# One unit's transposes in 64-row halves, another unit's second product in float32 by two column halves

## Chip, cores and metric

The kernel runs on one core of a Trainium2 chip. The metric is the device time of one execution in microseconds (us); lower is better.

## What is computed

Clustered attention and two dense blocks behind it, in float32. Queries and keys (2 batches, 8 heads, 768 positions, 64 wide) are each put to the nearest of 16 centroids of their head; a query sees the keys of its own cluster.

```python
mask = q_assign[:, :, :, None] == k_assign[:, :, None, :]
scores = np.where(mask, scale * np.matmul(q, k.transpose(0, 1, 3, 2)), -1000000000.0)
attn = np.exp(scores - np.max(scores, axis=-1, keepdims=True))
attn = attn / (np.sum(attn, axis=-1, keepdims=True) + 1e-09)
x = np.matmul(attn, v)                      # then (1536, 512)
h = np.maximum(x @ w_in, 0.0)
x = h * h @ w_out                           # first block, d_ff 2048
h = x @ w2_in
out = (h * np.clip(h + 3.0, 0.0, 6.0) / 6.0) @ w2_out
```

## The kernel before

Precision comes from splitting: a float32 operand is kept as a rounded high part and the remaining low part, both of the type fp32r, and a product is made of high by high, high by low and low by high.

The attention is done in 8 units, each one batch and two heads. A unit has 12 tiles: for each head 6 tiles of 128 queries against all 768 keys. Three tiles make a group, with 384 queries. For tile `n` the steps are

- `emit_qk` (L901, L904): the scores, two products of 384 columns by two terms, the second term with the mask rows;
- `emit_max` (L910, DVE) and `emit_exp` (L921, ACT, with a record that reads the accumulated sum): the exponentials `e` of [128 queries, 768 keys] in float32;
- `emit_tr` (L939): `e` transposed by PE in six blocks of 128 x 128, three for each `half` of the keys, into a bank of PSUM (`t`, three buffers that other steps share). The half is then split into `eh` and `el` either by ACT and DVE (L949, L950), or, for the tiles in `ON_POOL`, by a copy `et` (ACT, or DVE for `ET_DVE`) and two POOL operations (L377, L947);
- `emit_av` (L966): for each chunk `part` of 128 keys two products, the stationary operand being V's high and low parts side by side (64 + 64 columns), the moving one `eh`, then `el`; `emit_u` adds the two halves of the output's partitions.

The order is written out by hand. `schedule` runs for each tile `n` the places 0, 1, 1.5, 1.7, 2, 3, 4; between them stand `emit_tr(n, 0)` (after place 0), `emit_exp(n + 1)`, `emit_qk(n + 2)`, `emit_max(n + 2)` and `emit_tr(n, 1)` (after place 2). The tables `STEPS` and `FIRST` give the tile and place of each preparation step (loads, transposes of q and k `tq`, similarities `tsim`, their transposes `tas` of 64 rows, one-hot rows `toh`, mask rows `mt`, V's split in `vsplit`, the final scaling with `tn`), and `AV` gives the places of a group's six parts and of `emit_u`, counted from the group's first tile:

```python
AV = ((3, 3), (3, 4), (4, 1.7), (5, 0), (5, 1.7), (5, 2), (5, 2))
```

Each engine works through its instructions in this order. The loads and the transfers that build the stacked operands `op` all go through SP's queue. The steps of unit 0 stand in `OPENING`, with fill products on PE (`idle`, L783; `IDLE = (2, 3, 4)` gives their number at three places). Behind the attention the two dense blocks follow, in an order set by a planner (`Plan`), which the diff does not touch.

Of the kernel before, what the change touches and what calls it, by code (L numbers as in the profile page):

```python
# [9 lines left out]
F32 = mybir.dt.float32  # L10
F32R = mybir.dt.float32r
# [5 lines left out]
I32 = mybir.dt.int32  # L17

WARM = 10
FILL = {(0, 0): 1, (0, 1): 1, (1, 0): 1, (1, 1): 1, (2, 0): 1, (2, 1): 2, (3, 0): 2, (3, 1): 2}  # L20
IDLE = (2, 3, 4)

# [61 lines left out]
        "norm1": (17, 0),  # L84
    },
    2: {
        "load q": (-18, 1.5),
        "load k": (-17, 2),
        "load v": (-8, 1),
        "sim0": (-11, 0),  # L90
# [237 lines left out]
def cluster_attention_mlp_kernel(  # L328
# [38 lines left out]
    def f(ap):  # L367
        return ap.bitcast(F32)
# [78 lines left out]
    with ExitStack() as actx:  # L447
# [116 lines left out]
        def prep(u):  # L564
# [172 lines left out]
            def vsplit(half):  # L737
                if half == 0:
                    vst[u] = vs_p.tile([P, R, 2, 2 * D], F32R, tag="vs", name="vs")
                hs = slice(3 * half, 3 * half + 3)  # L740
                vr = raw[u, "v"][:, hs].rearrange("p r h d -> p (r h) d")
                tt = vst[u][:, hs].rearrange("p r h d -> p (r h) d")
                if E_VH == "p":
                    pool_round(tt[:, :, 0:D], vr)
                elif E_VH == "v":
                    nc.vector.tensor_copy(tt[:, :, 0:D], vr)
                else:
                    nc.scalar.activation(tt[:, :, 0:D], vr, AF.Copy)
                (nc.gpsimd if E_VL == "p" else nc.vector).tensor_sub(tt[:, :, D:], vr, f(tt)[:, :, 0:D])
# [20 lines left out]
            def first():  # L770

                h = ((0, 3), (3, 6))
                held = {}

                def hold(k, fn, *args):
                    held[k] = fn(*args)

                def idle(n):
                    if not n:
                        return  # L780
                    wt = ps_t.tile([P, 512], F32, tag="t", name="warm")
                    for _ in range(n):
                        nc.tensor.matmul(  # L783
                            wt[:, :HS], C[:, 0, 0:P], st["H"][:, 0, :HS], start=True, stop=True
                        )

                def table():
                    warm = sm_p.tile([P, 1], F32, tag="warm", name="warm", bufs=1)
                    nc.scalar.activation(warm, three, AF.Exp)

                steps = {
                    "q0": lambda: hold("q0", transp, 0, 0, True),
                    "cent": lambda: centroid_operands(cent),
                    "q0 split": lambda: held.pop("q0")(),
                    "k0": lambda: hold("k0", transp, 1, 0, True),
                    "k0 split": lambda: held.pop("k0")(),
                    "q1": lambda: hold("q1", transp, 0, 1, True),
                    "q1 split": lambda: held.pop("q1")(),
                    "k1": lambda: hold("k1", transp, 1, 1, True),
                    "k1 split": lambda: held.pop("k1")(),  # L800
                    "sim00": lambda: sims(0, 0),
                    "sim01": lambda: sims(0, 1),
                    "sim10": lambda: sims(1, 0),
                    "sim11": lambda: sims(1, 1),
                    "stack0": lambda: stack(0),
                    "stack1": lambda: stack(1),
                    "load k": lambda: load(1, "k"),
                    "load v": lambda: load(0, "v"),
                    "table": table,
                    "assign0": lambda: assign(*h[0]),  # L810
                    "lead0": lambda: leader(*h[0], 0),
                    "hot0": lambda: onehot(*h[0], 0),
                    "mask0": lambda: mask0(*h[0]),
                    "assign1": lambda: assign(*h[1]),
                    "lead1": lambda: leader(*h[1], 0),
                    "hot1": lambda: onehot(*h[1], 0),
                    "mask1": lambda: mask0(*h[1]),
                    "near0": lambda: emit_qk(0, 0),
                    "near1": lambda: emit_qk(1, 0),
                    "score0": lambda: emit_qk(0, 1),  # L820
                    "score1": lambda: emit_qk(1, 1),
                    "max0": lambda: emit_max(0),
                    "max1": lambda: emit_max(1),
                    "exp0": lambda: emit_exp(0),
                    "next q0": lambda: hold("next q0", prep_step, 1, "q0"),
                    "next q0 split": lambda: held.pop("next q0")(),
                    "next q1": lambda: hold("next q1", prep_step, 1, "q1"),
                    "next q1 split": lambda: held.pop("next q1")(),
                    "idle a": lambda: idle(IDLE[0]),
                    "idle b": lambda: idle(IDLE[1]),  # L830
                    "idle c": lambda: idle(IDLE[2]),
                }
                for k in OPENING:
                    steps[k]()
# [91 lines left out]
        def emit_tr(n, half):  # L926
            u, i, r = tile_of(n)
            g = n // 3
            if n % 3 == 0 and half == 0:
                eg[g] = (  # L930
                    eg_p.tile([P, R, HS], F32R, tag="eh", name="eh"),
                    eg_p.tile([P, R, HS], F32R, tag="el", name="el"),
                )
# [6 lines left out]
            qs = slice((n % 3) * P, (n % 3) * P + P)  # L940
            ks = slice(half * 3, half * 3 + 3)
            eh, el = eg[g][0][:, ks, qs], eg[g][1][:, ks, qs]
            if (n % (2 * R), half) in (ON_POOL_FIRST, ON_POOL_SECOND, ON_POOL, ON_POOL_LAST)[u if u < 2 else 3 if u == NU - 1 else 2]:
                et = e_p.tile([P, 3, P], F32, tag="et", name="et")
                copy((n % (2 * R), half) in (ET_DVE_FIRST, ET_DVE_SECOND, ET_DVE, ET_DVE_LAST)[u if u < 2 else 3 if u == NU - 1 else 2], et, t)
                pool_round(eh, et)
                nc.gpsimd.tensor_sub(el, et, f(eh))  # L947
            else:
                nc.scalar.activation(eh, t, AF.Copy)  # L949
                nc.vector.tensor_sub(el, t, f(eh))  # L950
            if half == 1:
                E_t.pop(n)

        A_t = {}

        def emit_av(g, part):

            u, i, r = tile_of(3 * g)
            if part == 0:
                A_t[g] = ps_a.tile([P, 512], F32, tag="a", name="a")  # L960
            a = A_t[g]
            eh, el = eg[g]
            vs = vst[u]
            for kr in (part,):
                for x in (eh, el):
                    nc.tensor.matmul(  # L966
                        a[:, :HS], vs[:, kr, i, :], x[:, kr, :],
                        start=(kr == 0 and x is eh), stop=(kr == R - 1 and x is el),
                    )
# [951 lines left out]
```

## Time and profile before

| what | us |
|---|---|
| median of 3 runs (lowest to highest) | 762.22 (761.32 to 763.06) |
| the profiled execution, its own time | 762.97 |
| its span, first to last instruction | 761.2 |
| PE busy | 751.7 |
| DVE, ACT, POOL busy | 606.3, 515.4, 481.4 |
| granted clock of TensorE, mean | 1.000 |

The span lies 1.8 us under the execution's own time. In the rows, PE is the matrix engine and PEld its loading of the stationary operand, which overlaps; the ends of PE's instructions are modelled, so starts say more than busy time.

### The profile page before, as it was taken

To read this page: it belongs to the slowest core of one execution; us is meant where nothing else is said; L and a number is where in the kernel's file an instruction comes from. 1 tells how busy PE (TensorE), PEld (TensorE's weight loads), DVE (VectorE), ACT (ScalarE), POOL (GpSimd) and SP (SyncE) were. 2 spreads that over 40 slices of the span, in tenths; PEclk is the share of its full clock that TensorE was granted. 3 is DMA by queue.
4 is the path that set the end of the run, shared out by engine and by line. 5 is a ranking of instruction groups with operands and counts; after the bars stand their busy time and mean duration, and the time that the engine had idled before them with its cause. 6 is when DMAs were issued, how large, how long until landed. Compare 5 with 4: busy or idle time off the path is not lost.

```text
span 761.2 us, 13022 instructions
## 1 busy us (share of the span) xinstructions
PE 751.7 (99%) x4438; PEld 711.2 (93%) x4438; DVE 606.3 (80%) x1068; ACT 515.4 (68%) x1100; POOL 481.4 (63%) x598
## 2 busy tenths in 40 slices
PE   8989999999999999999999999999999999999998
PEld 7888999999999999999999999999999899988998
DVE  6979999999998699878678776889657777776365
ACT  5889898898998777664554545677667555564461
POOL 2767888898897589963631743799464273166433
PEclk9999999999999999999999999999999999999999
DMA  8767738648432031222212122002212223200013
GB/s 183 163 131 162 153 70 183 136 96 187 112 83 70 1 112 56 84 84 70 94 59 84 56 84 84 28 29 85 83 57 67 73 84 108 86 29 29 1 41 125
DMA packets 62353, 66.96 MB, mean 88 GB/s; under 512 B 41200, under 2 KB 42736, under 8 KB 62288
## 3 DMA queue, kind: packets, MB, share of 16 engines
q1 hardware_dynamic: 61088, 65.85, 32.1%
q8 instruction: 35, 0.57, 0.3%
q10 hardware_dynamic: 1200, 0.30, 0.2%
q14 instruction: 30, 0.25, 0.1%
HBM read 43.02 MB, written 3.15 MB: 61 GB/s over the span
## 4 chain that ended last, share of the span: by engine, by line
PE 87%; POOL 7%; ACT 2%; issue 2%; DMA 2%; DVE 0%; SPq 0%; POOLq 0%; ACTq 0%
PE b L1407 27%; PE b L1489 16%; PE b L1528 15%; PE a L966 7%; PE t L939 6%; PE s L904 3%; PE s L901 3%; PE b L1770 2%; POOL el L947 2%; PE b L1665 2%; PE tsim L646 2%; PE tq L588 1%; POOL eh L377 1%; POOL xl L1018 1%; ACT e L921 1%
## 5 line engine op out<-in xcount | busy, mean ns | idle before, releaser
L1395 DVE TENSOR_TENSOR b<-b,tmp 128x384 f32<-128x384 f32 x84 | 47.4, 566 | 76.2 <-PE b L1407 31.1
L1205 POOL TENSOR_TENSOR s<-wt,s 128x256 fp32r<-128x256 f32 (+1 forms) x68 | 69.2, 1024 | 45.6 <-ACT s L1203 37.7
L939 PE MATMUL t<-ident,e 128*128 128x128 f32 x576 | 93.4, 275 | 1.2 <-ACT e L921 0.5
L910 DVE TENSOR_REDUCE nm<-s 128x1 f32<-128x768 f32 x96 | 90.6, 944 | 2.5 <-PE s L904 2.5
L947 POOL TENSOR_TENSOR el<-et,eh 128x384 fp32r<-128x384 f32 x84 | 86.1, 1024 | 7.0
L1391 ACT ACTIVATE tmp<-b 128x384 f32<-128x384 f32 x84 | 41.2, 491 | 71.8 <-PE b L1407 71.4
L921 ACT ACTIVATE e<-s,nm 128x768 f32<-128x768 f32 x96 | 86.6, 902 | 1.6 <-DVE nm L910 0.9
L1205 POOL TENSOR_TENSOR w<-wt,w 128x256 fp32r<-128x256 f32 (+1 forms) x48 | 43.3, 911 | 61.6 <-ACT w L1203 53.9
L939 PEld LDWEIGHTS t<-ident,e 128*128 128x128 f32 x576 | 70.3, 140 | 11.4 <-ACT e L921 4.5
L1188 POOL TENSOR_SCALAR wr<-wr 128x512 f32<-128x512 f32 x60 | 40.4, 674 | 62.3 <-DMA wr<-in_moe_w_in_dram 40.9
L966 PE MATMUL a<-eh,vs 128*128 128x384 f32 x192 | 70.0, 365 | 0.4 <-POOL xh L377 0.4
L377 POOL TENSOR_SCALAR eh<-et 128x384 fp32r<-128x384 f32 x84 | 45.2, 538 | 33.3 <-ACT et L374 29.5
L1407 PE MATMUL b<-xh,s 128*128 128x384 f32 x224 | 66.2, 336 | 0.0
L1407 PE MATMUL b<-xh,w 128*128 128x384 f32 x224 | 66.2, 336 | 0.0
L966 PE MATMUL a<-el,vs 128*128 128x384 f32 x192 | 64.8, 338 | 0.1
L950 DVE TENSOR_TENSOR el<-t,eh 128x384 fp32r<-128x384 f32 x108 | 58.8, 548 | 4.8 <-ACT eh L949 3.3
L949 ACT ACTIVATE eh<-t 128x384 fp32r<-128x384 f32 x108 | 52.8, 492 | 11.4 <-PE t L939 9.7
L901 PE MATMUL s<-op 128*128 128x384 f32 x188 | 55.4, 376 | 0.0
L1377 ACT ACTIVATE tmp<-b,three 128x384 f32<-128x384 f32 x64 | 37.0, 581 | 26.7 <-DVE b L1395 22.9
L1489 PE MATMUL b<-gA,s 128*128 128x384 f32 x276 | 54.2, 334 | 0.0
L904 PE MATMUL s<-op 80*128 80x384 f32 x192 | 49.7, 339 | 2.0 <-DMA op<-mt 1.9
L1192 DVE TENSOR_SCALAR b<-wr 128x512 int32<-128x512 int32 x60 | 41.3, 688 | 13.0 <-ACT wr L1191 12.2
(268 smaller groups left out, 2217.8 us busy)
## 6 DMA issues: line engine op xcount, KB each, us to landing
wr<-in_moe_w_out_dram SPq DMA_DIRECT2D x32, 512.0 KB, 3.2
op<-HL SPq DMA_DIRECT2D x82, 192.0 KB, 4.7
wr<-in_moe_w_in_dram SPq DMA_DIRECT2D x28, 512.0 KB, 3.5
rawv<-in_v_dram SPq DMA_DIRECT2D x16, 192.0 KB, 3.9
rawq<-in_q_dram SPq DMA_DIRECT2D x14, 192.0 KB, 4.2
rawk<-in_k_dram SPq DMA_DIRECT2D x14, 192.0 KB, 4.5
wr<-in_moe_w_in_dram SPq DMA_DIRECT2D x8, 256.0 KB, 2.9
op<-xh SPq DMA_DIRECT2D x8, 192.0 KB, 4.0
```

What stands on the lines that cost most here:

```text
L901: nc.tensor.matmul(s[:, h, :HS], o[:, 0, rs], o[:, 2, hs], start=True, stop=False)
L904: nc.tensor.matmul(s[:, h, :HS], o[0:80, 1, rs], o[0:80, 3, hs], start=False, stop=True)
L910: nc.vector.tensor_reduce(nm, S_t[n][:, :, :HS], axis=AX.XY, op=ALU.max, negate=True)
L921: nc.scalar.activation(e, s[:, :, :HS], AF.Exp, bias=nm, accum_out=sums[u][:, i * R + r : i * R + r + 1])
L939: nc.tensor.transpose(t[:, c, :], E_t[n][:, half, c * P : (c + 1) * P], ident)
L947: nc.gpsimd.tensor_sub(el, et, f(eh))
L950: nc.vector.tensor_sub(el, t, f(eh))
L966: nc.tensor.matmul(a[:, :HS], vs[:, kr, i, :], x[:, kr, :], start=(kr == 0 and x is eh), stop=(kr == R - 1 and x is el),)
L1205: pool(n / 365, lambda: nc.gpsimd.tensor_sub(lo, x, f(hi)), k + hk, lk)
L1407: nc.tensor.matmul(h, w[:, a, cc], x[b][:, cc], start=(first and n == 1), stop=(n == 6 * len(terms)), skip_group_check=not first,)
L1489: nc.tensor.matmul(o, x[:, ds], y, start=(fb == 0 and k == 0), stop=(fb == NF - 1 and k == 2))
L1528: nc.tensor.matmul(o, g[:, ts], w[:, ns], start=(fb == 0 and k == 0), stop=(fb == NF - 1 and k == 2),)
```

## The change

- `emit_tr_rows` takes the place of `emit_tr` in unit 3: at place 0 of a tile all 768 keys are transposed by twelve transposes of 64 query rows each, alternating between the upper and the lower 64 rows, into two banks; each bank holds 64 queries by all 6 chunks and is split as before, with rows of 64 elements. At the place of the second half nothing is done.
- In unit 4 `emit_tr` only copies its half to `eh` (ACT for the first, DVE for the second), `vsplit` only copies V, and `emit_av_full` multiplies in float32: at the odd parts two products of 64 output columns, one chunk into output partitions 0 to 63, the next into 64 to 127. At the even parts nothing is done.
- The last four fill products of the opening become float32 products on 64 rows, alternating between the halves and between two banks.
- Unit 2's "load q" goes from tile 6, place 1.5 (18 tiles ahead of its unit) to tile 0, place 0 (24 ahead).

PE in unit 3, tiles 2 and 3 (the line numbers of the change differ). Before:

```order
L939 MATMUL t<-ident,e 128x128 x3
L901 MATMUL s<-op 128x384 x2
L904 MATMUL s<-op 128x384 x2
L966 MATMUL a<-eh,vs 128x384
L966 MATMUL a<-el,vs 128x384
L966 MATMUL a<-eh,vs 128x384
L966 MATMUL a<-el,vs 128x384
L939 MATMUL t<-ident,e 128x128 x3
L665 MATMUL tas<-ident,sim 128x64 x6
```

and in the change:

```order
L985 MATMUL t<-ident,e 128x64 x12
L915 MATMUL s<-op 128x384 x2
L918 MATMUL s<-op 128x384 x2
L1033 MATMUL a<-eh,vs 128x384
L1033 MATMUL a<-el,vs 128x384
L1033 MATMUL a<-eh,vs 128x384
L1033 MATMUL a<-el,vs 128x384
L667 MATMUL tas<-ident,sim 128x64 x6
L985 MATMUL t<-ident,e 128x64 x12
```

The second three transposes of the tile have gone to its beginning, and twelve of 64 rows stand there together; "tas", which already had 64 rows, comes to stand next to the following tile's twelve.

ACT in unit 3, from the copy of its first tile's first half on (`e,sums` is the exponential, `lo` and `tmp` belong to preparation and to `emit_u`). Before:

```order
L374 ACTIVATE et<-t 128x384
L921 ACTIVATE e,sums<-s,nm 128x768
L949 ACTIVATE eh<-t 128x3x128
L374 ACTIVATE lo<-tsim 64x384
L921 ACTIVATE e,sums<-s,nm 128x768
```

and in the change:

```order
L376 ACTIVATE et<-t 128x384
L1000 ACTIVATE eh<-t 128x6x64
L935 ACTIVATE e,sums<-s,nm 128x768
L376 ACTIVATE lo<-tsim 64x384
L1000 ACTIVATE eh<-t 128x6x64
```

The copy of the tile's second part has gone from behind the next tile's exponential to in front of it.

SP's queue in unit 0, from the load of unit 0's V on (`op<-mt` are mask rows; `op<-xh` and `op<-xl` are unit 1's stacked operands). Before:

```order
L494 DMA rawv<-in_v_dram 128x6x64 x2
L733 DMA op<-mt 16x768 x2
L621 DMA op<-xh 64x768
L622 DMA op<-xh 64x768
L623 DMA op<-xh 64x768
```

and in the change:

```order
L496 DMA rawv<-in_v_dram 128x6x64 x2
L496 DMA rawq<-in_q_dram 128x6x64 x2
L735 DMA op<-mt 16x768 x2
L623 DMA op<-xh 64x768
L624 DMA op<-xh 64x768
```

The load of unit 2's q stands ahead of unit 0's mask rows; before, it stood behind them and behind all of unit 1's stacked operands.

The diff:

```diff
--- before.py
+++ after.py
@@ -17,6 +17,8 @@
 I32 = mybir.dt.int32
 
 WARM = 10
+TR_ROWS = 3
+AV_FULL = 4
 FILL = {(0, 0): 1, (0, 1): 1, (1, 0): 1, (1, 1): 1, (2, 0): 1, (2, 1): 2, (3, 0): 2, (3, 1): 2}
 IDLE = (2, 3, 4)
 
@@ -84,7 +86,7 @@
         "norm1": (17, 0),
     },
     2: {
-        "load q": (-18, 1.5),
+        "load q": (-24, 0),
         "load k": (-17, 2),
         "load v": (-8, 1),
         "sim0": (-11, 0),
@@ -740,6 +742,9 @@
                 hs = slice(3 * half, 3 * half + 3)
                 vr = raw[u, "v"][:, hs].rearrange("p r h d -> p (r h) d")
                 tt = vst[u][:, hs].rearrange("p r h d -> p (r h) d")
+                if u == AV_FULL:
+                    nc.gpsimd.tensor_copy(f(tt)[:, :, 0:D], vr)
+                    return
                 if E_VH == "p":
                     pool_round(tt[:, :, 0:D], vr)
                 elif E_VH == "v":
@@ -779,7 +784,16 @@
                     if not n:
                         return
                     wt = ps_t.tile([P, 512], F32, tag="t", name="warm")
-                    for _ in range(n):
+                    for k in range(n):
+                        if n == 4:
+                            rs = slice(64 * (k % 2), 64 * (k % 2) + 64)
+                            if k == 0:
+                                w2 = ps_t.tile([P, 512], F32, tag="t", name="warm2")
+                            nc.tensor.matmul(
+                                (w2 if k % 2 else wt)[:, :HS], f(C)[rs, 0, 0:P],
+                                f(C).rearrange("p a b -> p (a b)")[rs, :HS], start=True, stop=True,
+                            )
+                            continue
                         nc.tensor.matmul(
                             wt[:, :HS], C[:, 0, 0:P], st["H"][:, 0, :HS], start=True, stop=True
                         )
@@ -926,6 +940,10 @@
         def emit_tr(n, half):
             u, i, r = tile_of(n)
             g = n // 3
+            if u == TR_ROWS:
+                if half == 0:
+                    emit_tr_rows(n)
+                return
             if n % 3 == 0 and half == 0:
                 eg[g] = (
                     eg_p.tile([P, R, HS], F32R, tag="eh", name="eh"),
@@ -940,7 +958,9 @@
             qs = slice((n % 3) * P, (n % 3) * P + P)
             ks = slice(half * 3, half * 3 + 3)
             eh, el = eg[g][0][:, ks, qs], eg[g][1][:, ks, qs]
-            if (n % (2 * R), half) in (ON_POOL_FIRST, ON_POOL_SECOND, ON_POOL, ON_POOL_LAST)[u if u < 2 else 3 if u == NU - 1 else 2]:
+            if u == AV_FULL:
+                copy(half, f(eh), t)
+            elif (n % (2 * R), half) in (ON_POOL_FIRST, ON_POOL_SECOND, ON_POOL, ON_POOL_LAST)[u if u < 2 else 3 if u == NU - 1 else 2]:
                 et = e_p.tile([P, 3, P], F32, tag="et", name="et")
                 copy((n % (2 * R), half) in (ET_DVE_FIRST, ET_DVE_SECOND, ET_DVE, ET_DVE_LAST)[u if u < 2 else 3 if u == NU - 1 else 2], et, t)
                 pool_round(eh, et)
@@ -951,13 +971,60 @@
             if half == 1:
                 E_t.pop(n)
 
+        def emit_tr_rows(n):
+            g = n // 3
+            if n % 3 == 0:
+                eg[g] = (
+                    eg_p.tile([P, R, HS], F32R, tag="eh", name="eh"),
+                    eg_p.tile([P, R, HS], F32R, tag="el", name="el"),
+                )
+            ts = [ps_t.tile([P, 512], F32, tag="t", name="t") for _ in range(2)]
+            for c in range(R):
+                for x in range(2):
+                    rs = slice(64 * x, 64 * x + 64)
+                    nc.tensor.transpose(
+                        ts[x][:, 64 * c : 64 * c + 64],
+                        E_t[n][rs, c // 3, (c % 3) * P : (c % 3) * P + P],
+                        ident[rs, rs],
+                    )
+            for x in range(2):
+                t = ts[x][:, :HS].rearrange("p (c q) -> p c q", c=R)
+                qs = slice((n % 3) * P + 64 * x, (n % 3) * P + 64 * x + 64)
+                eh, el = eg[g][0][:, :, qs], eg[g][1][:, :, qs]
+                if (n % (2 * R), x) in ON_POOL:
+                    et = e_p.tile([P, R, 64], F32, tag="et", name="et")
+                    copy((n % (2 * R), x) in ET_DVE, et, t)
+                    pool_round(eh, et)
+                    nc.gpsimd.tensor_sub(el, et, f(eh))
+                else:
+                    nc.scalar.activation(eh, t, AF.Copy)
+                    nc.vector.tensor_sub(el, t, f(eh))
+            E_t.pop(n)
+
         A_t = {}
+
+        def emit_av_full(g, part):
+
+            u, i, r = tile_of(3 * g)
+            a = A_t[g]
+            eh = f(eg[g][0])
+            vs = f(vst[u])
+            if part % 2 == 0:
+                return
+            for kr in (part - 1, part):
+                x = kr % 2
+                nc.tensor.matmul(
+                    a[64 * x : 64 * x + 64, :HS], vs[:, kr, i, 0:D], eh[:, kr, :],
+                    start=part == 1, stop=part == 5, skip_group_check=True,
+                )
 
         def emit_av(g, part):
 
             u, i, r = tile_of(3 * g)
             if part == 0:
                 A_t[g] = ps_a.tile([P, 512], F32, tag="a", name="a")
+            if u == AV_FULL:
+                return emit_av_full(g, part)
             a = A_t[g]
             eh, el = eg[g]
             vs = vst[u]
```

## Rows read from the trace of the kernel before

**Rows 1.** Windows, units 3, 4: us, busy us of PE, PEld, DVE, ACT, POOL.

```profile
108.30:137.84 29.54, 29.51 (x205) 27.81 (x204) 28.30 (x51) 26.87 (x61) 26.45 (x37) 1.00 0.62 137
137.84:167.40 29.56, 29.55 (x205) 27.80 (x204) 28.17 (x49) 26.88 (x61) 26.02 (x36) 1.00 0.64 137
```

**Rows 2.** Windows, unit 3, exponentials (L921) alone: two records a tile.

```profile
108.30:137.84 29.54, 11.92 (x24) 1.00 0.62 137
```

**Rows 3.** Timeline of PE in one tile of unit 3: start us, us, instructions.

```profile
122.82 0.49 PE L939 MATMUL t<-ident,e 128*128 128x128 f32 x3
123.07 0.60 PE L901 MATMUL s<-op 128*128 128x384 f32 x2
...
124.04 0.34 PE L966 MATMUL a<-el,vs 128*128 128x384 f32 x1
124.21 0.34 PE L966 MATMUL a<-eh,vs 128*128 128x384 f32 x1
```

**Rows 4.** Timeline of PE around the 64-row transposes "tas".

```profile
117.05 0.49 PE L939 MATMUL t<-ident,e 128*128 128x128 f32 x3
117.47 0.59 PE L665 MATMUL tas<-ident,sim 64*128 64x64 f32 x6
...
118.29 0.60 PE L901 MATMUL s<-op 128*128 128x384 f32 x2
```

**Rows 5.** Timeline of PEld around the same; in brackets idle time before.

```profile
117.46 0.45 PEld L665 LDWEIGHTS tas<-ident,sim 64*128 64x128 f32 x6 [0.17 <-issue]
```

**Rows 6.** Tile tas: duration ns min/median/max, first and last start.

```profile
L665 PEld LDWEIGHTS tas<-ident,sim x48: 135/138/140, 9.8 to 206.4; 64*128 64x128 f32 x48
L665 PE MATMUL tas<-ident,sim x48: 222/223/273, 9.8 to 206.5; 64*128 64x64 f32 x48
...
  issue: 1.4, 8
```

**Rows 7.** Timelines: the transposes of one half (PE), then ACT behind them.

```profile
120.11 0.49 PE L939 MATMUL t<-ident,e 128*128 128x128 f32 x3
...
120.69 0.49 ACT L374 ACTIVATE et<-t 128x384 f32<-128x384 f32 x1 [0.37 <-PE t L939]
121.08 0.90 ACT L921 ACTIVATE e<-s,nm 128x768 f32<-128x768 f32 x1
121.87 0.20 ACT L921 ACTIVATION_READ_ACCUMULATOR e<-s,nm 128x1 f32 x1
```

**Rows 8.** Opening: PE timeline, ACT timeline, and two pieces of the chain.

```profile
15.70 1.39 PE L783 MATMUL warm<-HL,c 128*128 128x384 f32 x7
...
17.11 0.55 PE L939 MATMUL t<-ident,e 128*128 128x128 f32 x3
...
16.06 0.90 ACT L921 ACTIVATE e<-s,nm 128x768 f32<-128x768 f32 x1
...
18.12 4.29 DMA rawv<-in_v_dram
...
25.72 0.79 PE a L966 x3
```

**Rows 9.** SP issues, the PE wait for the mask rows, and time to landing.

```profile
35.33 2.12 SPq L494 DMA_DIRECT2D rawq<-in_q_dram  x2
...
41.06 2.92 SPq L733 DMA_DIRECT2D op<-mt  x4
...
45.99 0.59 PE L904 MATMUL s<-op 80*128 80x384 f32 x2 [1.94 <-DMA op<-mt]
...
op<-mt SPq DMA_DIRECT2D x30, 48.0 KB, 2.2
```

**Rows 10.** Groups of the page: busy us, mean ns of one | idle us.

```profile
L939 PE MATMUL t<-ident,e 128*128 128x128 f32 x576 | 93.4, 275 | 1.2 <-ACT e L921 0.5
...
L947 POOL TENSOR_TENSOR el<-et,eh 128x384 fp32r<-128x384 f32 x84 | 86.1, 1024 | 7.0
...
L950 DVE TENSOR_TENSOR el<-t,eh 128x384 fp32r<-128x384 f32 x108 | 58.8, 548 | 4.8 <-ACT eh L949 3.3
```

## The prediction

> **What bounds the kernel now.** I read first the windows, cut at the start of each unit's exponentials. Unit 3 takes 29.54 us and unit 4 29.56 us, and PE is busy for 29.51 and 29.55 of them; DVE for about 28.2, ACT 26.9, POOL 26 [rows 1]. The stretch holds 24 records of the exponential, two a tile, so 12 tiles: 2.46 us a tile [rows 2]. A busy PE may only look full, so I then took the pitches, from start to start, out of PE's timeline. A 384-column fp32r product takes 0.17 to 0.18 us (124.04 to 124.21), say 0.175 [rows 3]. Three float32 transposes last 0.49 us as a group and 0.275 each [rows 3, 10], so the second and third add (0.49 - 0.275) / 2 = 0.11 each; that is the pitch. A tile has 6 transposes and 8 products: 0.66 + 1.40 = 2.06 us. The rest, 0.40 us a tile, is other units' preparation and merging: 18 more transposes (2.0), 8 similarity products (1.4) and a few small ones, about 4.2 us a unit. 12 x 2.06 + 4.2 = 28.9 of 29.5. **PE is the bound in both units, with about half a microsecond to spare.** What lies behind the attention is also a chain of PE, so what PE loses or gains in units 3 and 4 goes through to the end.
>
> It follows that the relief of the other engines in unit 4 is worth nothing: about half of its splits no longer have a low part on POOL (1.02 us each) and half none on DVE (0.55) [rows 10], and the float32 copy of V has one POOL operation less a half. All of that lay beside PE.
>
> **A price that the kernel before does show: changing the array's shape.** Once a unit, six transposes of 64 rows ("tas") stand among transposes of 128 rows. The three before them start at 117.05, so the array is free at 117.05 + 3 x 0.11 = 117.38. The six loads last 0.45 us as a group, 0.138 each, so the pitch is (0.45 - 0.138) / 5 = 0.062 [rows 5, 6]; they need 0.37. From the first of three transposes to the next product is 0.25 us (122.82 to 123.07) [rows 3]. So the product should start at 118.00; it starts at 118.29 [rows 4]. **0.29 us are lost by going to 64 rows and back**, and PEld stands idle 0.17 us of it for "issue", which is no wait that the profile shows; that comes 8 times, 1.4 us in all [rows 5, 6].
>
> **Unit 3, transposes.** Twelve of 64 rows take the place of six of 128 in each tile, in one go, with products on both sides. Removed: 0.66 us. Added: 0.29 for the two changes of shape, and twelve transposes. If the upper and lower half run one after the other, these are 12 x 0.062 = 0.74 us; if each pair runs at once, 0.37. No row shows two halves at work together; the only sequence of 64-row transposes has them all in one half, at 0.062 [rows 5], and I take 0.062. PE then needs 0.37 us more a tile, 12 x 0.37 = 4.5 us, less 0.29 where "tas" stands next to a burst: 4.2.
>
> There is a second cost. ACT takes its work in the order of the program. Before, one half's copy stood ahead of the next tile's exponential; now both halves do, and the next tile's transposes wait for that exponential. The loop: the last transpose of the first half starts about 0.05 + 10 x 0.062 = 0.67 us after the first and lasts 0.22 [rows 6]; the copy starts 0.09 behind it (120.60 to 120.69), 0.98; copy to copy and copy to exponential are 0.39 each (120.69 to 121.08), 1.76; the exponential with its read of the sum takes 0.99 (121.08 to 122.07) [rows 7], 2.75; the transposes start 0.06 later (the opening: 16.06 + 0.99 = 17.05 against 17.11 [rows 7, 8]). That is 2.81 us. PE alone needs 2.06 + 0.37 = 2.43 in a tile without preparation. Four tiles (0, 3, 6, 8) have none, and wait 0.38 each: 1.5 us. Before, the same loop with one copy and 3 transposes was about 2.0 us, under PE's 2.06. **Unit 3: +5.7 us**; bounds +1.9 (pairs at once, worked out below) and about +6.
>
> **Unit 4, second product.** Before, two chunks are four fp32r products, 0.70 us. Now they are two float32 products of 384 columns, with 64 output columns, and a change of shape around them: the parts 1, 3 and 5 of each group carry two chunks, so 3 bursts a group and 12 in the unit. No row shows a float32 product. Bounds: the float32 transpose costs 0.11 per 128 columns, so 0.33 for 384; and twice that, 0.66, if both operands are split in two and not only the data of a transpose. I take 0.66, nearest to the four fp32r terms (0.70) that a product of two halves by two halves would be. The Trainium skill's page "FP8 and Floating Point Precision" (TensorE Precision Notes) counts four passes for a true FP32 product, by which the sum stands as I take it. If the two chunks, in the two halves of the output's partitions, run together, a burst is 0.29 + 0.66 = 0.95, 0.25 more than before; 12 x 0.25 = 3.0 us. They also fall unevenly: one burst in the first tile of three, none in the second, two in the third. The second then has PE work of 0.66 + 0.70 = 1.36 us, less than the loop through ACT of about 2.0, which wastes some 0.1 to 0.6 a group where no preparation fills it; +0.5. **Unit 4: +3.5 us**; if the two run one after the other, 12 x 0.66 = 7.9 more, +11.4; at 0.33 and together, 0.5 - 12 x 0.08 = -0.5.
>
> **Opening.** Four fill products (0.70 us) become four float32 ones on 64 rows: two pairs, 2 x 0.66 + 0.29 = 1.6 us. The seven before began at 15.70 and the transposes at 17.11 waited for the exponential that ends at 17.05 [rows 8]; now they start some 0.6 us later (1.9 if nothing overlaps). Until 25.72 the chain runs through the load of V and POOL [rows 8], so I cost this at 0; without that cover it is 0.6 to 1.9.
>
> **The load of unit 2's q** goes from in front of the mask rows' transfers (35.33) to a place after the first load of V, where SP waits anyway. PE later waits 1.94 us for mask rows issued from 41.06 on, behind that traffic; such a transfer usually lands 2.2 us after issue [rows 9]. With 2.1 us of issues less ahead they can be earlier by 0 to 1.5 us; the mask must first be written. I take 0.8.
>
> **Sum:** 5.7 + 3.5 + 0 - 0.8 = +8.4 us on the profiled execution's 762.97 (span 761.2): 771.4. That execution lies 0.75 above the median of the runs shown, 762.22, so the forecast for a median is **770.6 us**.
>
> **Rivals.**
> - *Both kinds of halves run together.* Unit 3: PE needs 0.37 + 0.29 = 0.66 a tile as before, but ACT's loop is 2.81 - 0.37 = 2.44 against 2.06 in the four light tiles and 2.39 in five with a little preparation: 4 x 0.38 + 5 x 0.05 = 1.8. Sum 1.8 + 3.5 - 0.8 = +4.5, **766.7**. For it: the instructions alternate between the halves and write different banks. Against: 0.062 is more than half of 0.11, so part of the price may be the instruction itself, which doubles. The Trainium skill's page "TensorE: Matmul & The Clock Gate" (Part 3) gives a speed-up of about 3 for four row tiles at once, which would make this the case; no run here shows it yet.
> - *Neither runs together.* 5.7 + 11.4 + 0.5 in the opening - 0.8 = +16.8, **779.0**.
> - *Unit 4's halves one after the other, unit 3's together:* 1.8 + 11.4 - 0.8 = +12.4, 774.6.
> - *Faster: the change of shape is free when products stand on both sides*, and halves run together. Unit 3's transposes are 0.37 instead of 0.66; its loop is 2.3 us, so most of that is not used: about -0.3. Unit 4: 12 x (0.66 - 0.70) = -0.5. With 1.5 from the load: -2.3, **759.9**. It decides at a price of about 0.12 us per change and back: (24 x 0.12 is about 2.9, some of it hidden in unit 3). Against it: 0.29 in a row where nothing was waited for.
> - *The change does little*, because float32 products are cheap (0.33) and the loop through ACT is loose: within 1.5 us, 762.
>
> **Chances.** Forecast 0.40, both together 0.22, neither 0.20, mixed 0.06, faster 0.06, little 0.06. About 0.2% (1.5 us) is what a measurement of this kernel can tell from no change. So faster 0.06, same 0.06, slower 0.88. The range goes from 764.5, below the case of both together, to 780.5, over most of that of neither.
>
> **What would show it.** Right: units 3 and 4 take about 35 and 33 us, the others 29.5; in unit 3 LDWEIGHTS of 64 rows at a pitch near 0.06 in bursts of 12, "issue" before each burst, and the transposes waiting for ACT's exponential in light tiles; in unit 4 pairs of float32 products that start within 0.1 us of each other and hold PE for about 0.95 us. Wrong: a pitch near 0.03 in unit 3; float32 products 0.66 us apart (779); or no gap at the changes of shape.

## The result, and the profile after

| what | before, us | change, us |
|---|---|---|
| median of 3 runs (lowest to highest) | 762.22 (761.32 to 763.06) | 768.02 (767.90 to 769.26) |
| the profiled execution | 762.97 | 767.90 |
| its span | 761.2 | 766.1 |
| from the first exponential of unit 0 to that of unit 2 | 62.46 | 61.49 |
| unit 3 | 29.54 | 33.43 |
| units 4 and 5 together | 59.13 | 61.84 |

The change is **slower: 1.0068 times the time of before, interval 1.0043 to 1.0092**. By medians that is 5.8 us, between the two profiled executions 4.9. A unit reaches, as in [rows 1], from the start of its exponentials to that of the next unit's. Unit 4's last products fall into unit 5's window, so these two are taken together. Unit 2 is as before (29.77 after 29.78), and so is unit 6. The sum over the units: unit 3 +3.9, units 4 and 5 +2.7, units 0 and 1 together -1.0. Another 0.7 us is gained before unit 0's first exponential, ahead of everything that the change touches; that start lies between 15.4 and 16.8 us over the profiles of this study, so it is chance. Three executions of this study, the profiled one of e2 among them, took 1235 to 1903 us and enter no ratio.

The windows of the change, in the columns of [rows 1]; units 3, 4, 5:

```profile
106.62:140.06 33.44, 31.39 (x281) 26.41 (x280) 29.44 (x52) 27.27 (x63) 26.50 (x37) 1.00 0.56 121
140.06:171.15 31.09, 30.86 (x201) 23.17 (x199) 26.16 (x45) 22.94 (x51) 11.03 (x16) 1.00 0.62 130
171.15:201.90 30.75, 30.61 (x205) 25.64 (x204) 28.04 (x47) 26.39 (x61) 22.26 (x31) 1.00 0.62 132
```

Against [rows 1], PE now stands idle for 2.05 us of unit 3, where it was idle for 0.03. In unit 4 it has stayed full: POOL's work fell from 26.0 to 11.0 us and PE's time rose.

**A light tile of unit 3**, the change's answer to [rows 3]: timeline of PE and, last, the loads of PEld.

```profile
122.26 0.58 PE L985 MATMUL t<-ident,e 64*128 64x64 f32 x12
122.78 0.62 PE L915 MATMUL s<-op 128*128 128x384 f32 x2
123.23 0.51 PE L918 MATMUL s<-op 80*128 80x384 f32 x2
...
124.11 0.33 PE L1033 MATMUL a<-el,vs 128*128 128x384 f32 x1
124.68 0.58 PE L985 MATMUL t<-ident,e 64*128 64x64 f32 x12 [0.24 <-ACT e L935]
...
122.26 0.45 PEld L985 LDWEIGHTS t<-ident,e 64*128 64x128 f32 x12 [0.25 <-ACT u L396]
```

Twelve loads take 0.45 us, as long as six did in [rows 5]: **the upper and the lower half run at once**. The single records show it: the two of a pair start 3 to 4 ns apart, and twelve starts span 0.36 us. The price of the changed shape is there too. The last product before a burst is followed after 0.27 us instead of 0.175, the first pair takes 0.11 instead of 0.06, the last transpose 0.15 instead of 0.06, and the first product 0.28 instead of 0.175: 0.34 us, against the 0.29 read from "tas". A burst without waits costs six pairs at 0.062 and 0.34, together 0.71 us of PE; the six transposes of before cost 0.66. By this the form of the transposes is almost neutral, and most of the 3.9 us must be waits.

What ended the idle time of PE and of PEld before the twelve, both added up, and how often (the view of line L985):

```profile
  ACT e L935: 3.6, 8
  DVE HL L599: 1.0, 2
  issue: 0.8, 3
  ACT et L376: 0.6, 2
  DVE el L1001: 0.4, 1
```

Two things are late. One is the next tile's exponential, as at 124.68, where the transposes start 0.06 us after ACT has read the sum. The other is a **bank of PSUM**: `HL`, `et` and `el` are written by the instructions that empty a bank of `t`. The twelve transposes need two of the three banks at once, and `tq`, `tsim` and the others use the same three. In four tiles the second half starts 0.27, 0.37, 0.51 and 0.69 us after the first for want of a bank, 1.8 us together; the bank comes free with an `el`, an `et`, an `et` of unit 2's last tile, and an `HL`. PE's starts in unit 3 have eight gaps above 0.3 us; before there was one. Four of the eight stand between the last product and a burst: 0.57, 0.58, 0.66 and 0.77 us, where a burst without a wait has 0.27, so 1.5 us too much. They end with the exponential, the longest with a bank just behind it. The account closes: 12 x 0.05 for the form, 1.5 ahead of bursts and 1.8 inside them make 3.9.

**A burst of unit 4**, PE and the load of its products:

```profile
150.52 0.55 PE L957 MATMUL t<-ident,e 128*128 128x128 f32 x3
151.00 0.87 PE L1016 MATMUL a<-eh,vs 128*64 128x384 f32 x4
151.80 0.55 PE L957 MATMUL t<-ident,e 128*128 128x128 f32 x3
...
151.00 0.20 PEld L1016 LDWEIGHTS a<-eh,vs 128*64 128x64 f32 x4 [0.17 <-issue]
```

Two float32 products show as four records. The two halves of the output's partitions start 6 to 7 ns apart, the second records 0.37 us after the first. The last transpose before them starts at 150.80, so the array is free at 150.91; the second transpose behind them starts at 151.96, one pitch of 0.11 after 151.85. A burst takes the 0.95 us between, as forecast, against 0.70 for the four products of before; 0.17 of it is again "issue".

**The mask rows** of unit 1, SP's queue and the product that waited 1.94 us in [rows 9]:

```profile
35.56 2.03 SPq L496 DMA_DIRECT2D rawv<-in_v_dram  x2
37.69 1.96 SPq L496 DMA_DIRECT2D rawk<-in_k_dram  x2
41.38 2.49 SPq L735 DMA_DIRECT2D op<-mt  x4
...
44.29 0.59 PE L918 MATMUL s<-op 80*128 80x384 f32 x2
```

The wait is gone, though the first of the four transfers was issued at 41.38 instead of 41.06: SP waits for the mask. They **land sooner**: from issue to landing the first takes 2.15 us, before 4.6. The load of q is no longer in the traffic ahead of them; with that load alone moved (e4, below) it is 2.16.

### The profile page after: what moved, and what is told of

It is laid out like the page before. It is cut to its first block, busy times and chain, and to the rows that moved or that the text cites. A ratio compares the mean times of both kernels' runs of the same rounds, so it can differ in the third digit from the quotient of the medians.

```text
span 766.1 us, 13122 instructions
## 1 busy us (share of the span) xinstructions
PE 755.7 (99%) x4514; PEld 702.5 (92%) x4514; DVE 605.3 (79%) x1065; ACT 511.3 (67%) x1090; POOL 462.2 (60%) x574
## 4 chain that ended last, share of the span: by engine, by line
PE 83%; POOL 7%; ACT 3%; DMA 2%; issue 2%; DVE 1%; SPq 1%; POOLq 0%; ACTq 0%
PE b L1474 27%; PE b L1556 16%; PE b L1595 15%; PE a L1033 5%; PE t L957 5%; PE s L915 3%; PE s L918 2%; PE b L1837 2%; POOL el L967 2%; PE b L1732 2%; PE tsim L648 2%; ACT e L935 1%; POOL eh L379 1%; PE tq L590 1%; PE a L1016 1%
## 5 line engine op out<-in xcount | busy, mean ns | idle before, releaser
L957 PE MATMUL t<-ident,e 128*128 128x128 f32 x504 | 82.2, 276 | 1.5 <-ACT mt L723 0.5
L957 PEld LDWEIGHTS t<-ident,e 128*128 128x128 f32 x504 | 60.4, 140 | 16.5 <-ACT e L935 5.3
L967 POOL TENSOR_TENSOR el<-et,eh 128x384 fp32r<-128x384 f32 x62 | 63.6, 1025 | 5.2
L379 POOL TENSOR_SCALAR eh<-et 128x384 fp32r<-128x384 f32 x73 | 39.2, 537 | 39.8 <-ACT et L376 32.6
L1033 PE MATMUL a<-eh,vs 128*128 128x384 f32 x168 | 61.1, 364 | 0.4 <-POOL xh L379 0.4
L1033 PE MATMUL a<-el,vs 128*128 128x384 f32 x168 | 56.8, 338 | 0.3 <-POOL el L967 0.3
L1595 PE MATMUL b<-s,gA 128*128 128x512 f32 x198 | 49.4, 391 | 0.0
L1556 PEld LDWEIGHTS b<-gA,s 128*128 128x128 f32 x276 | 48.5, 188 | 0.0
```

Of the source, the lines that this page charges most:

```text
L957: nc.tensor.transpose(t[:, c, :], E_t[n][:, half, c * P : (c + 1) * P], ident)
L1033: nc.tensor.matmul(a[:, :HS], vs[:, kr, i, :], x[:, kr, :], start=(kr == 0 and x is eh), stop=(kr == R - 1 and x is el),)
L1556: nc.tensor.matmul(o, x[:, ds], y, start=(fb == 0 and k == 0), stop=(fb == NF - 1 and k == 2))
L1595: nc.tensor.matmul(o, g[:, ts], w[:, ns], start=(fb == 0 and k == 0), stop=(fb == NF - 1 and k == 2),)
```

## Experiments

The ratios are to the kernel before as measured beside each run, in three groups on three chips: 763.06 us for e1 to e4, 763.33 for e5 to e8, 764.52 for e9 to e12.

### Each part alone

**Unit 3 as before, the rest of the change kept** (e1_no_rows).

```diff
-TR_ROWS = 3
+TR_ROWS = -1
```

> The change without the 64-row transposes: unit 3 transposes as before, all else as changed. Theory (unit 3's 33.43 us against 29.54 is all due to its transposes): unit 3 back to 29.5 to 29.8 us, units 4 and 5 stay at 31.1 and 30.7, the time falls by 3.5 to 4 us, to about 764. Rival (unit 3 also pays for unit 4's new copies, whose V is prepared during unit 3): unit 3 stays above 30.3 and less than 3 us come back.

764.6 us, ratio 1.0014 (0.9999 to 1.0028). Unit 3 is back at 29.5:

```profile
106.91:136.46 29.55, 29.52 (x205) 27.81 (x204) 28.36 (x51) 26.89 (x62) 25.45 (x36) 1.00 0.63 137
```

Units 4 and 5 together are 62.2. All of unit 3's cost comes from its own transposes and the order that comes with them.

**Unit 4 as before, the rest kept** (e2_no_full, and again as e11_no_full, whose trace is shown).

```diff
-AV_FULL = 4
+AV_FULL = -1
```

> The change with unit 4's second product as before (fp32r, four products for two chunks); all else as changed. Theory (12 bursts at 0.95 us take the place of 0.70): units 4 and 5 go back from 31.1 and 30.75 to 29.6 each, unit 3 stays at 33.4, the time falls by 2.5 to 3 us. Rival (the relief of ACT, DVE and POOL in unit 4 is worth something, so the burst costs more than it seems): units 4 and 5 fall by less than 1.5 together, or unit 3 grows because V's low part is back on POOL.

> The same kernel as the run with unit 4's second product as before, for its trace. Theory (units 3 and 4 cost apart): unit 3 at 33.4, units 4 and 5 at 29.6 each, about 3 us under the change. Rival (unit 3 gains from unit 4's lighter engines or loses to its copies): unit 3 differs from 33.4 by over 0.5 us.

764.7 us both times, ratios 1.002 (1.0006 to 1.0034) and 1.0008 (0.9989 to 1.0026). Windows of units 3, 4, 5 in the second:

```profile
106.84:140.26 33.42, 31.36 (x281) 26.38 (x280) 29.41 (x52) 27.29 (x63) 27.58 (x38) 1.00 0.61 121
140.26:169.41 29.15, 29.13 (x201) 27.27 (x200) 27.92 (x48) 26.53 (x60) 24.88 (x34) 1.00 0.65 138
169.41:198.97 29.56, 29.52 (x205) 27.82 (x204) 28.18 (x48) 26.91 (x61) 26.39 (x37) 1.00 0.66 137
```

Unit 3 keeps its 33.4, and units 4 and 5 take 58.7 instead of 61.84. The float32 product costs 3.1 us beside this unit 3, and the two costs are separate.

**The load of q put back** (e3_old_load), and **the kernel before with the load moved alone** (e4_only_load).

```diff
     2: {
-        "load q": (-24, 0),
+        "load q": (-18, 1.5),
```

> The change with the load of unit 2's q back at its old place. Theory: PE waits again some 1.5 to 2 us for the mask rows near 44 us, and the time grows by 1.0 to 1.7 us. Rival (the wait vanished by the run's own variation in transfers): PE's wait for the mask rows stays under 0.5 us and the time is the same within 0.5.

> The kernel before with the moved load alone. Theory: 1.0 to 1.7 us faster than before, ratio near 0.998, with no wait for the mask rows. Rival: the time is the kernel before's within 0.5 us, because the wait comes back elsewhere in unit 1 (POOL's low parts bound that stretch).

Put back: 772.23 us, ratio 1.012 (1.0096 to 1.0143), which is 4.2 us more than the change and more than was expected. Alone: **761.78 us, ratio 0.9981 (0.9969 to 0.9993)**, 1.3 us by medians; it beats both kernels, and units 0 and 1 take 60.97 instead of 62.46. Its PE does not wait for the mask rows:

```profile
44.31 0.59 PE L904 MATMUL s<-op 80*128 80x384 f32 x2
```

In the first of the two, PE and then the windows of 45 to 50 and 50 to 60 us:

```profile
47.15 0.59 PE L918 MATMUL s<-op 80*128 80x384 f32 x2 [2.64 <-DMA op<-mt]
...
50.52 0.84 PE L918 MATMUL s<-op 80*128 80x384 f32 x2
51.16 0.52 PE L1033 MATMUL a<-eh,vs 128*128 128x384 f32 x1
```

```profile
45.00:50.00 5.00, 2.85 (x16) 2.79 (x17) 1.89 (x3) 1.39 (x4) 2.94 (x4) 0.86 0.28 65
50.00:60.00 10.00, 10.00 (x62) 9.72 (x61) 8.30 (x15) 7.95 (x18) 5.83 (x9) 0.90 0.46 101
```

The wait for the mask rows is 2.64 us here, and behind it the granted clock falls from the upper to the lower of its two levels (2.4 and 1.2 GHz) for a stretch: from the two products at 50.52 to the next instruction at 51.16 are 0.64 us, 0.32 a product instead of the 0.175 of [rows 3]. Behind the wait of 1.94 us in the kernel before [rows 9] it did not fall. Units 0 and 1 take 65.44 us here instead of 61.49, so 4.0 of the 4.2 us lie in them: 2.64 are the wait, and the stretch at the lower clock behind it is the likely rest. Why the wait is 0.7 us longer than before was not tried; the mask rows are issued 1.1 us later (42.13 against 41.06).

The clock also has a part in what the moved load gains. In 12 of the 29 executions of the kernel before in this group the mean granted clock was below 0.999, and they took 764.9 us at the median; the other 17 took 762.5. With the load alone that was so in 2 of 12 executions, and the other ten took 761.7: at an equal clock the load gains 0.8 us, and the rest of the 1.3 is a clock that falls less often. Over all groups the mean was below 0.999 in 33 of 64 executions with the load at its old place, all 4 of e3 among them, and in 6 of 71 with it at its new one (counting those that enter a ratio; e5 and e6 are left out, whose traces show the fall elsewhere). Where the clock fell in executions without a trace is not known.

**Before with the load and the float32 fill products** (e12_load_fill; the load's line and the opening's piece of the diff).

```diff
-        "load q": (-18, 1.5),
+        "load q": (-24, 0),
...
+                        if n == 4:
+                            rs = slice(64 * (k % 2), 64 * (k % 2) + 64)
...
```

> The kernel before with the moved load and the four float32 fill products on 64 rows, nothing else. Theory (the fill is covered until the load of V ends): the start of unit 1's exponentials stays at 46.6 to 47.1 us, as with the moved load alone, and the time within 0.7 us of it. Rival (the first transposes and all behind them start 0.6 us later): unit 1 starts at 47.3 or later.

761.75 us, ratio 0.9966 (0.9949 to 0.9983), beside 761.78 for the load alone: the fill costs nothing that can be measured. In the profiled execution, at 763.26 above the median, unit 1 starts at 47.94, on the rival's side of the mark; but the granted clock was 0.92 in its first 16 us, so this trace does not decide. The trace of the change does, whose opening has the same fill:

```profile
15.62 1.68 PE L792 MATMUL warm<-c 64*128 64x384 f32 x8
...
17.39 0.52 PE L957 MATMUL t<-ident,e 128*128 128x128 f32 x3
```

The first exponential starts at 15.37 there, so the first transposes come 2.0 us behind it, where they came 1.05 behind it before (16.06 and 17.11, [rows 8]). This 1.0 us does not last: the exponentials of unit 1 start at 46.64 in the change and at 46.67 with the load alone.

### What unit 3 pays for

**Both halves' transposes and copies at the tile's beginning, but in 128 rows** (e9_whole_rows): the order of the change without its shape.

```diff
                 if half == 0:
-                    emit_tr_rows(n)
+                    emit_tr_half(n, 0)
+                    emit_tr_half(n, 1)
                 return
+            emit_tr_half(n, half)
+
+        def emit_tr_half(n, half):
...
```

`emit_tr_half` is the body that `emit_tr` has for the other units.

> The change, with unit 3's transposes of 128 rows again, but both halves of the keys together at the tile's start and both copies ahead of the exponential, as the 64-row form has them. No change of shape, no pairs. Theory (unit 3's cost is the order: everything of a tile at its start, two banks and two copies at once, so that the next transposes wait for ACT and for a bank): unit 3 still takes 32 to 33.5 us. Rival (the cost is the change of shape, 12 x 0.29 us): unit 3 goes back to 29.5 to 30.3.

767.13 us, ratio 1.0035 (1.0023 to 1.0048). Unit 3's window, then its first two waits (us, times, longest):

```profile
107.00:139.31 32.31, 30.95 (x208) 27.95 (x207) 29.61 (x52) 27.27 (x62) 26.59 (x37) 1.00 0.62 125
```

```profile
PEld t L963 <- ACT e L935: 2.2, 4, 0.8
ACT eh L975 <- PE t L963: 1.9, 6, 0.6
```

Unit 3 takes 32.31: **2.8 of the 3.9 us come from the order alone**, with the same transposes as before. The order by itself also stops two tiles between their halves, for 0.39 and 0.45 us where the pitch is 0.11. The 64-row form with its changes of shape adds the other 1.1.

**The copies of the second half behind the next tile's exponential** (e5_copy_later). `split_rows(n, x)` is the loop body of `emit_tr_rows` that empties bank `x`.

```diff
                 if half == 0:
                     emit_tr_rows(n)
+                else:
+                    split_rows(n, 1)
                 return
...
-            for x in range(2):
-                t = ts[x][:, :HS].rearrange("p (c q) -> p c q", c=R)
+            rows_t[n] = ts
+            split_rows(n, 0)
...
```

> The change, with the copies of a tile's second 64 queries (unit 3) put behind the next tile's exponential, where the second half's copies stood before; the twelve transposes stay together. Theory A (unit 3 waits for ACT: two copies stand ahead of the exponential that the next transposes need): the four waits of 0.3 to 0.4 us for the exponential go, and unit 3 falls from 33.4 to about 32.4 us or less. Theory B (unit 3 waits for a PSUM bank that DVE's subtraction frees): the banks now come free later still, and unit 3 stays at 33.4 or grows.

773.78 us, ratio 1.0126 (1.0042 to 1.0209), from two executions, of which the profiled one, 774.9 us, also ran part of its opening at the lower clock. In unit 3 the clock is at 1.00, and the unit grows to 36.2; units 4 and 5 grow too, to 63.3, for a reason that stays open. Unit 3's window, and what the twelve now waited for:

```profile
109.49:145.72 36.23, 32.70 (x278) 26.55 (x277) 29.04 (x51) 27.16 (x62) 26.05 (x37) 1.00 0.52 112
```

```profile
  ACT et L376: 3.0, 7
  DVE HL L599: 1.0, 2
  issue: 1.0, 4
  DVE el L1010: 0.8, 2
  ACT mt L723: 0.8, 2
  PE toh L717: 0.8, 1
  ACT e L935: 0.8, 3
```

The exponential's share falls from 3.6 to 0.8 us, as meant, and the banks' rises by more: nine of the twelve bursts now stop between the first and the second half, for 0.27 to 0.92 us. The ACT loop is not the whole story; what ACT does later comes back as a bank that is free later.

**The first half's bank always emptied by one ACT copy, the rest on POOL** (e6_bank_early).

```diff
-                if (n % (2 * R), x) in ON_POOL:
+                if x == 0:
                     et = e_p.tile([P, R, 64], F32, tag="et", name="et")
-                    copy((n % (2 * R), x) in ET_DVE, et, t)
+                    copy(False, et, t)
```

> The change, with the first 64 queries of every tile of unit 3 copied out by ACT and split on POOL, the second by ACT and DVE: the first bank is free after one copy. Theory B (the second transposes of a burst wait for a bank that DVE frees, 1.8 us in the unit): these waits go, unit 3 falls by 1 to 2 us to 31.5 to 32.5. Theory A (ACT's order): unit 3 stays within 0.5 us of 33.4.

773.54 us, ratio 1.0122 (1.0068 to 1.0177), from two executions: neither number. All of unit 3, and a stretch in it:

```profile
106.72:145.82 39.10, 34.06 (x281) 28.33 (x280) 28.57 (x48) 28.21 (x64) 28.30 (x40) 0.91 0.51 104
124.00:136.00 12.00, 9.50 (x62) 7.18 (x61) 6.89 (x11) 6.52 (x15) 8.47 (x13) 0.72 0.41 87
```

The first six bursts take as long as in the change (108.28 to 124.65, there 108.20 to 124.68). Of the two stops between halves in them, the one of 0.51 us stays, since a copy of unit 2's last tile ends it; the one of 0.27 goes, but PE's wait for the exponential ahead of that burst grows from 0.25 to 0.33. Then POOL is the bound. It has twelve halves to split at some 1.5 us each (0.54 for `eh`, 1.02 for `el` in the groups) and falls behind; PE waits 1.58 us for its `eh` at 128.07, the clock falls as in e3, the eleventh burst stops 1.79 us between its halves for a bank that an `HL` frees, and the unit is 5.7 us longer than in the change. So the run does not show what an earlier free bank is worth by itself, and a fourth bank for `t` was not tried.

**The lower half's six transposes behind the upper half's six** (e8_unpaired).

```diff
-            for c in range(R):
-                for x in range(2):
+            for x in range(2):
+                for c in range(R):
```

> The change, with the six transposes of the upper 64 queries all ahead of the six of the lower (unit 3): no neighbours in different halves. Theory (a pair costs 0.062 because its two run at once): the burst takes 0.37 us longer, in all tiles where PE is the bound, and unit 3 grows by 2.5 to 4.5 us. Rival (instructions are issued ahead far enough that the halves overlap anyway, or waits have hidden the difference): unit 3 grows by less than 1 us.

768.26 us, ratio 1.0066 (1.0044 to 1.0087); unit 3 is 33.91, +0.5.

```profile
122.54 0.77 PE L985 MATMUL t<-ident,e 64*128 64x64 f32 x12
123.23 0.62 PE L915 MATMUL s<-op 128*128 128x384 f32 x2
...
125.10 0.95 PE L985 MATMUL t<-ident,e 64*128 64x64 f32 x12 [0.19 <-DVE xx L1080]
```

In the burst at 122.54 the starts are 0.54 us apart from first to last instead of 0.36. The single records make two trains with a pitch of 0.062 each; the second begins 0.18 us after the first, before its fourth transpose. So the halves overlap even when they are listed apart, and across the two halves PE does not start its transposes in the order of the program. Only where the second half's bank was not free, in three of the twelve bursts, does one run behind the other: 0.73 us from the first start to the last at 125.10, where an `el` frees the bank at 125.42, and 0.87 in the other two.

### What unit 4 pays for

**One burst a group instead of three** (e7_one_burst): six products at the place of the last part, to pay the change of shape once.

```diff
-            if part % 2 == 0:
+            if part < 5:
                 return
-            for kr in (part - 1, part):
+            for kr in range(6):
...
-                    start=part == 1, stop=part == 5, skip_group_check=True,
+                    start=kr < 2, stop=kr > 3, skip_group_check=True,
```

> The change, with all six float32 products of a group in unit 4 at one place (where the third burst stands): 4 changes of shape and back instead of 12. Theory (the cost of unit 4 is the change of shape, 0.29 us each): 8 x 0.29 = 2.3 us less, units 4 and 5 together at about 59.5 instead of 61.85. Rival (the cost is in the uneven load, which one burst makes worse): no gain, 61.5 or more.

768.2 us, ratio 1.007 (1.0053 to 1.0088). Units 4 and 5, then PE behind one burst:

```profile
140.59:171.27 30.68, 28.73 (x193) 23.25 (x191) 25.57 (x44) 22.98 (x51) 11.18 (x16) 1.00 0.63 131
171.27:202.67 31.40, 31.27 (x213) 26.43 (x212) 28.41 (x49) 26.43 (x60) 22.29 (x31) 1.00 0.60 129
```

```profile
155.16 2.16 PE L1016 MATMUL a<-eh,vs 128*64 128x384 f32 x12
157.24 0.88 PE L957 MATMUL t<-ident,e 128*128 128x128 f32 x6
...
159.58 0.55 PE L957 MATMUL t<-ident,e 128*128 128x128 f32 x3 [0.27 <-ACT e L935]
```

62.1 against 61.84: no gain. Eight changes of shape at 0.29 are saved, about 2.3 us by count, but PE, idle for 0.23 us of unit 4 in the change, is now idle for 1.95: in tiles without a burst it waits three times 0.27 to 0.33 us for ACT's exponential and once 0.91 for an ACT instruction of the preparation (`w`). Here the records of one half follow each other at 0.32 us, so **a float32 product of 384 columns costs 0.64 us**, 3.7 times the 0.175 of one in fp32r. The Trainium skill's page "FP8 and Floating Point Precision" (TensorE Precision Notes) counts four passes for it. The trace nearly agrees: four at 0.175 would be 0.70.

**One burst in every tile** (e10_even), instead of one, none and two.

```diff
+                if g // 4 == AV_FULL:
+                    av = (av[0], (3, 4), av[2], (4, 3), av[4], (5, 2), av[6])
```

> The change, with the second of a group's three float32 bursts in unit 4 moved one tile earlier, so that each of three tiles has one. As many changes of shape as before. Theory (0.25 us a burst for shape and products, 3.0 us, is the floor, and the rest is unevenness): little changes, units 4 and 5 together at 61.3 to 61.9. Rival (uneven load is the larger part): 60.8 or less.

767.92 us, ratio 1.0047 (1.0028 to 1.0066).

```profile
140.04:171.13 31.09, 30.86 (x201) 23.17 (x199) 26.19 (x46) 22.97 (x51) 11.08 (x16) 1.00 0.59 130
171.13:201.80 30.67, 30.67 (x205) 25.64 (x204) 27.79 (x47) 26.42 (x61) 21.96 (x31) 1.00 0.63 132
```

61.76 against 61.84: this other spacing of the bursts is worth 0.1 us. Twelve times 0.25 is 3.0 us, nearly all of the 3.1 of unit 4.

## Why the prediction was right, and which step failed

- **PE is the bound, and the relief of the other engines is worth nothing: right.** POOL's work in unit 4 fell by 15 us and the unit became longer. In unit 3 PE did not stay the bound: it is idle for 2.05 us there.
- **The change of shape costs about 0.3 us: right.** 0.34 in unit 3 and 0.3 in unit 4 (the burst's 0.95 less 0.64), with "issue" as the only sign in the profile's views. "Tas", which the prediction took it from, was a fair row for both.
- **Unit 3, +5.7, measured +3.9. This step failed**, at "If the upper and lower half run one after the other, these are 12 x 0.062 = 0.74 us; if each pair runs at once, 0.37 ... I take 0.062." They run at once, at 0.36, so PE's own cost is 0.05 us a tile instead of 0.37, in the unit 0.6 instead of 4.2. The prediction gave "a pitch near 0.03 in unit 3" as a sign of being wrong, and this is it; the rival of both halves together had it, and its 766.7 lies 1.3 us from the median measured, the forecast 2.6. (Its unit 3 is 1.8 by its own terms; the 1.9 among the bounds is the same sum.) The loop through ACT was right: 1.5 forecast, and 1.5 of waits ahead of four bursts measured. At nothing, in the forecast and in the rival, stood the banks: `emit_tr_rows` takes two of three buffers of `t` in one go, which was to be read in the code, and the four stops between the halves are 1.8 us. The Trainium skill's page "TensorEngine Tiling (Array Packing)" (Gotcha 1: PSUM Pressure) says that different row tiles write to different PSUM banks. The trace agrees in that the second half stops for a bank of its own; e9 adds that two banks at once stop some tiles without row tiles too. Taken from the other side, the order alone, which the prediction priced at 1.5, cost 2.8 (e9), and the rest 1.1. So unit 3 came within 1.8 us by luck, through two errors of opposite sign: 3.6 too much for PE's own work, 1.8 too little for the banks.
- **Unit 4, +3.5, measured +2.7 against before and +3.1 against e11.** The burst of 0.95 us, the product of 0.66 (0.64) and the two halves at once were right. The 0.5 for uneven bursts was too much: 0.1 (e10). The same loop through ACT shows only when the bursts are three times as long (e7).
- **Opening, 0: right.** The first transposes start 1.0 us later, not 0.6, and the load of V covers it: unit 1 starts as early as without the fill.
- **Load of q, -0.8, measured -1.3** (e4), within its bounds of 0 to -1.5, and -0.8 among the executions whose clock did not fall. The way was half wrong: the mask rows' transfers are not issued earlier, the first lands 2.5 us sooner after issue.
- **The sum:** -1.0 + 3.9 + 2.7 = +5.6 between the profiles, less the 0.7 at the start that is chance, is the 4.9 seen; by medians +5.8, forecast +8.4 (770.6 against 768.0).

## What to carry to other kernels

Before two steps are drawn together, count what they hold in common, here the PSUM banks, and what then stands ahead of the next tile's first instruction on each engine: the order cost more than the new instructions. Smaller array shapes do run side by side, but each excursion of a full-sized stream into another shape cost about 0.3 us here, so bursts of this size, 0.66 us of transposes or 0.70 of products, had nothing to win. A load moved away from the front of a transfer that is waited for is worth trying by itself: it was the only part of this change that gained.

## What the runs showed of the hardware

- Transposes of 64 rows in the two halves of the array start 3 to 4 ns apart and each half keeps its 0.062 us a transpose, so two halves do twice the work of one. Listed one half after the other, the second half's first still starts before the first half's fourth (e8).
- Two float32 products into the two halves of PSUM's partitions start 6 to 7 ns apart; each shows as two records, 0.37 us apart in a burst of two and 0.32 farther on in a burst of six (e7).
- A wait of PE of 2.64 us was followed by some microseconds at the lower clock (e3), one of 1.94 in the same place was not in the one trace of it [rows 9]. With the load at its old place the mean granted clock was below 0.999 in 33 of 64 executions, at its new one in 6 of 71 (e5 and e6 left out).
- The first of the same four transfers took 2.15 us to land (2.16 in e4) or 4.6 (4.4 in e3), with another load out of the traffic ahead of them or in it.
